# Two value-into-weight foldings per row of small products in the second stage

## The chip, the cores and the metric

One Trainium2 chip, one core. The metric is device time of one execution in microseconds (us); lower is better.

## What is computed

For each of 8 batches of 576 tokens (4608 tokens, 8 heads of 64, width 512) a linear attention with 32 memory slots is computed, and its result goes through two feed-forward layers:

```python
a = softmax over s of phi;  k_m, v_m = a.T @ k, a.T @ v      # per batch and head: 32 x 64
p = softmax((q @ k_m.T) / 8)                                  # per head: 576 x 32
x = concat over heads of p @ v_m                              # 4608 x 512
x = (silu(x @ w_gate) * (x @ w_val)) @ w_out                  # d_ff 1536
out = elu(x @ w_in) @ w_out2                                  # d_ff 2048
```

All is float32. Products that must be exact to float32 are done as three fast products of a high and a low part (`hi*hi + hi*lo + lo*hi`).

## The kernel before, in words

The kernel never forms `p @ v_m`. Since `(p @ v_m) @ w` is `p @ (v_m @ w)`, it folds the 32x64 values of each head into the gate and value weights first. One **folding** (`vw`, line 253) serves one batch `b` and one **unit pair** `p`: two hidden units of 128, gate and value, 512 columns. It is a row of eight small products (64 rows by 32 columns of the array each, one for each head, line 260). They are plain float32, and each shows as two instructions, so a folding is 16 matmul records on line 260. The result fills a PSUM tile of two banks (`pvw`); ScalarE then copies it to a high part (line 265) and VectorE subtracts that from the PSUM tile to get the low part (line 266). Only after the subtraction is the PSUM tile free. `together` (line 95) keeps the products of one row next to each other in TensorE's order.

The program has three stages. The first (lines 593 to 670) does the attention and the first 4 hidden units of the first layer, batch by batch. **The second** (lines 676 to 853) does the other 8 hidden units, and that is where the change is. The third (from line 855) is the second layer.

The second stage goes over four pairs of batches `n`. In each pair there are 8 unit pairs, that is 16 units. A unit (`unit2`, line 698) is 12 matmuls `pg`, a Silu on ScalarE, 12 matmuls `pv`, and a multiplication on VectorE (line 703). After each second unit of `n` comes one folding for the unit pair two further on (line 828). The first 16 units run without output steps around them. From then on the units of `n + 1` are mixed with the 14 **output steps** of `n` (`step`, line 750): each step has two halves `hf`, each of 12 matmuls `acc` (lines 286 to 288), preceded by a high and low split of its input on ScalarE and VectorE (lines 767 and 768). This part is called the mixed stretch below. At the end the 14 steps of the last pair of batches run alone.

PSUM in the second stage: four two-bank tiles, numbered 0 to 3 (`bank2`, line 686). In the mixed stretch the output steps hold 2 and 3, while `pg`, `pv` and the foldings take turns on 0 and 1, in the order of the list `turn` (line 690). In the first 16 units, the units take turns on 0, 1 and 2 (the very first on 3), and foldings use 3 alone.

ScalarE and VectorE also convert the later weights from 64-bit words in the background (`load_w`, `set_split`; lines 127 to 132, 168 and 227 to 233), which fills what time they have left.

The order on each engine is set by a list scheduler while the program is built; it takes the ready instruction of the highest priority. `tc.issue_after(ins)` puts the instructions of a block behind `ins` on the same engine; `high_priority` moves them ahead. An output step is kept behind the unit before it (`behind`, line 754), but only the first three matmuls of a step are.

Of the kernel before, what the change touches and what calls it, by code (L numbers as in the profile page):

```python
# [8 lines left out]
F32 = mybir.dt.float32  # L9
F32R = mybir.dt.float32r  # L10
# [3 lines left out]
ALU = mybir.AluOpType  # L14
# [7 lines left out]
KD = DM // 128  # L22
# [16 lines left out]
def attention_moe_moe(ctx: ExitStack, tc: tile.TileContext, qT, phiT, kv, kv4, w1g, w1o, w2, out):  # L39
# [3 lines left out]
    stt = nc.vector.scalar_tensor_tensor  # L43
    mm = nc.tensor.matmul
# [5 lines left out]
    vx_p = ctx.enter_context(tc.tile_pool(name="vx", bufs=4))  # L50
# [33 lines left out]
    last, first = {}, {}  # L84
# [10 lines left out]
    def together(calls):  # L95
        first = calls[0]()
        with tc.issue_after(first.ins), tc.high_priority():
            for call in calls[1:]:
                call()
# [70 lines left out]
    WG = [[None] * KD for _ in range(NU1 // 2)]  # L170
# [77 lines left out]
    VW = {}  # L248
# [1 line left out]

    def vw(b, p, pool=None, ps=None):
        t = VW[b, p] = vx_p.tile([128, 2, 2, 512], F32R, tag="vx", name="vw")
        both = ps or pool.tile([128, 2, 512], F32, tag="at", name="pvw")
        ps = [both[:, g] for g in range(2)]

        def head(j, g):
            r, c = slice(64 * g, 64 * g + 64), slice(32 * j, 32 * j + 32)
            return mm(ps[g][c], lhsT=Bs[b].vt[r, j, :], rhs=WG[p][j][r], start=True, stop=True)  # L260

        together([lambda j=j, g=g: head(j, g) for j in reversed(range(KD)) for g in (1, 0)])
        if b >= NEG or p >= UA // 2:
            with tc.high_priority() if pool is None else nullcontext():
                act(out=t[:, 0], in_=both, func=AF.Copy)
                tt(out=t[:, 1], in0=both, in1=t[:, 0].bitcast(F32), op=ALU.subtract)
            return
        for g in range(2):
            last["vwh"] = act(out=t[:, 0, g, :], in_=ps[g], func=AF.Copy)
        for g in range(2):  # L270
            mm(ps[g], lhsT=minus, rhs=t[:, 0, g, :], start=False, stop=True, skip_group_check=True)
            last["vwl"] = act(out=t[:, 1, g, :], in_=ps[g], func=AF.Copy)
            if g == 0:
                last["vwl0"] = last["vwl"]
# [10 lines left out]
    def down(ps, w, hs, ms, start, stop, skip=False):  # L285
        mm(ps, lhsT=w[0][:, ms], rhs=hs[0], start=start, stop=False, skip_group_check=skip)  # L286
        mm(ps, lhsT=w[1][:, ms], rhs=hs[0], start=False, stop=False, skip_group_check=skip)  # L287
        mm(ps, lhsT=w[0][:, ms], rhs=hs[1], start=False, stop=stop, skip_group_check=skip)  # L288

    def split_h(pool, h, n):  # L290
        hh = pool.tile([128, n], F32R, tag="hh", name="hh")
# [201 lines left out]
    Bs = [Batch(b) for b in range(B)]  # L493
# [99 lines left out]
    for b in range(B):  # L593
# [53 lines left out]
        hs = {}  # L647
        for hf in range(2):
            for u in range(UA):
                s = gate1(b, u, Bs[b].at, HS * hf, silu)  # L650
# [35 lines left out]
    def bank2(i, name):  # L686
        return (ps_3 if i == 3 else ps_2[i // 2]).tile([128, 2, T], F32, tag=f"g{i}", name=name)

    MIX = 1000
    turn = ([3, 0] + [1, 2, 0] * 10 + [1, 0] * MIX)[:32 + MIX]  # L690

    def up2(b, u, c, name):
        ps = bank2(turn.pop(0), name)
        for hf in range(2):
            up1(ps[:, hf, :HS], VW[b, u // 2], 256 * (u % 2) + c, at2[b], HS * hf)
        return ps[:, :, :HS]

    def unit2(b, u, out):
        pg = up2(b, u, 0, "pg")
        s = t_p.tile([128, 2, HS], F32, tag="s", name="s")  # L700
        last["gate"] = act(out=s, in_=pg, func=AF.Silu)
        pv = up2(b, u, 128, "pv")
        last["h"] = stt(out=out, in0=s, scalar=1.0, in1=pv, op0=ALU.mult, op1=ALU.mult)

    def vw2(b, p):
        if len(turn) > MIX:
            ps = bank2(3, "pvw")
        else:
            ps = bank2(turn.pop(0), "pvw")
        vw(b, p, ps=ps)  # L710


    held = {}
# [33 lines left out]
    def down_steps(n, g, steps, comb):  # L747
        acc = {}

        def step(j, name, r, k, chain, *dst):  # L750
            start = name in ("P1", "P2", "P5", "P4")[:4 if steps is ALONE else 3]
            if start and j == 0:
                acc[chain] = [bank2(i, "acc")[:, :, :HS] for i in ((0, 1) if chain == "D" else (2, 3))]
            behind = nullcontext() if steps is ALONE else tc.issue_after(unit_end[-LAG].ins)
            if steps is not ALONE:
                w = wo_p.tile([128, 2, 2, 256], F32R, tag="w", name="ws")
                nc.sync.dma_start(out=w.bitcast(F32), in_=d1_d[:, r, 2 * j:2 * j + 2])
            else:
                if j == 0:
                    acc["w"] = vx_p.tile([128, 4, 2, 256], F32R, tag="vx", name="ws")  # L760
                    last["ws"] = nc.sync.dma_start(out=acc["w"].bitcast(F32), in_=d1_d[:, r])
                w = acc["w"][:, 2 * j:2 * j + 2]
            for hf in range(2):
                hs = [hs_p.tile([128, 2, HS], F32R, tag=t, name=t) for t in ("hh", "hl")]
                x = g[k][:, hf, 2 * j:2 * j + 2]
                with tc.high_priority():
                    act(out=hs[0], in_=x, func=AF.Copy)  # L767
                    last["h"] = last["gate"] = tt(out=hs[1], in0=x, in1=hs[0].bitcast(F32), op=ALU.subtract)
                for o, a, b, f in comb.get((name, 2 * j + hf), []):
                    with tc.issue_after(last["h"].ins):  # L770
                        tt(out=g[o][:, f], in0=g[a][:, f], in1=g[b][:, f], op=ALU.add if (o, a, b) == (2, 2, 3) else ALU.subtract)
                for i, m in [(i, m) for i in range(2) for m in range(2)]:
                    with behind if hf + i + m == 0 else nullcontext():
                        down(acc[chain][m][:, hf], (w[:, i, 0], w[:, i, 1]), (hs[0][:, i], hs[1][:, i]),
                             slice(128 * m, 128 * m + 128), start and j + i == 0, j + i == 2, not start)
            if j == 1:
                add_part(acc[chain], [(2 * n + b, c) for b, c in dst],
                         name == "P4" if steps is ALONE else None)

        return [lambda a=a, j=j: step(j, *a) for a in steps for j in range(2)]  # L780

    def fetch_x():
# [19 lines left out]
    def background(fs, x):  # L802
        store_w2()
        while fs and len(fs) > x:
            fs.pop(0)()

    pairs = [(2 * n + bi, UA // 2 * (k + 1) + j) for n in range(B // 2) for k in range(2) for bi in range(2)
             for j in range(UA // 2)]
    load2(1)

    unit_end = []
    LAG = 1

    def units(n, g):
        fs, n0 = conv[n], len(conv[n])
        done = [0]

        def unit(i, k, u):
            b, p = pairs[8 * n + i]
            if u % UA == 0:  # L820
                g[k] = gh_p.tile([128, 2, UA, HS], F32, tag="gh", name="gh")
            unit2(b, u, g[k][:, :, u % UA])
            unit_end.append(last["pe"])
            done[0] += 1
            background(fs, n0 * (1 - done[0] / (12 if n == 0 else 16)))
            if u % 2 == 1:
                if 8 * n + i + 2 < len(pairs):
                    vw2(*pairs[8 * n + i + 2])
                if i in (5, 7) and n < B // 2 - 1:
                    load2(2 * n + 2 + i // 7, nc.gpsimd)  # L830

        return [lambda i=i, k=i // 2 % 2 * 2 + i // 4, u=2 * pairs[8 * n + i][1] + j: unit(i, k, u)
                for i in range(8) for j in range(2)]

    g = [{} for _ in range(B // 2)]
# [144 lines left out]
    for q in range(NQD):  # L980
        with tc.issue_after(last["ws"].ins):
            w = fetch(up_d[q][:, 2:6])
        ps = [bank((2 * q + i) % 6) for i in range(2)]
# [7 lines left out]
    for q in range(NQD):  # L991
        w = fetch(dn_d[q // 4][:, 2:6, q % 4])
# [21 lines left out]
    for t0 in range(T, NT, 2 * T):  # L1014
# [10 lines left out]
        def head(q):  # L1025
            z = Q[q]
            z["w0"] = fetch(up_d[q][:, :4])
            z["p1"], z["p5"] = bank(q % 2), bank(3 + 2 * (q % 2))
            product(q, "P1", z["p1"], True)
            with tc.high_priority():  # L1030
                z["s1"] = keep(z["p1"])
            product(q, "P5", z["p5"], True)
            with tc.high_priority():
                z["s5"] = keep(z["p5"])
# [43 lines left out]
        acc = {"D": [dbank(0), dbank(1)]}  # L1078
        K = {}
        for n, (name, r, slot) in enumerate(STEPS):  # L1080
# [3 lines left out]
            start = name in ("P1", "P2", "P5")  # L1084
            for p in range(NQD // 2):
                if p % 2 == 0:
                    w = fetch(dn_d[p // 2][:, r])
                g = G[p]
                hi, lo = split2(g[:, slot], op_p, ("hi", "lo"))
                if name in AFTER:  # L1090
                    o, a, b, op = AFTER[name]
# [10 lines left out]
            for mt in range(2):  # L1102
                ps = acc[chain][mt]
# [52 lines left out]
```

## Time and profile before

| | us |
|---|---|
| median of 3 runs | 1428.58 (1428.11 to 1428.69) |
| the profiled execution's own time | 1427.93 |
| its span | 1426.2 |
| TensorE matmul busy | 1401.3 (98%) |
| VectorE busy | 1136.1 (80%) |
| ScalarE busy | 862.4 (60%) |
| granted TensorE clock, mean of the span | 0.995 |

PE is TensorE's matmul side, PEld its weight loads, DVE is VectorE, ACT is ScalarE, POOL is GpSimd and SP the engine that issues most DMAs. Matmuls are pipelined: one starts while the one before still drains, so the time that a matmul costs is read from the distance between starts, not from its duration. In a timeline each row has the start and the duration in us, the engine, the source line, the operation, output<-inputs by name, and how many instructions were merged; in brackets stands the idle time before it and what ended that.

### The profile page before, as it was taken

The page shows a single profiled execution, that of the slowest core. Times are in us where ns is not written, and L with a number is a line of the kernel's source. Part 1 is how long each engine was busy: PE and PEld are TensorE (multiplying, and loading weights), DVE is VectorE, ACT ScalarE, POOL GpSimd, SP SyncE. Part 2 cuts the span into 40 slices and gives each one's busy share as a digit, 9 for nine tenths or more (in the row PEclk, how much of TensorE's full clock was granted, in tenths as well). Part 3 has the DMA queues.
Part 4 walks back from the last instruction along what each step waited for, and adds up shares of the span by engine and source line. Part 5 has one row for each costly group of instructions (what it writes and reads, how often), then busy time and mean ns, then how long its engine had stood idle before and what let it go on. Part 6 is the DMA issues. An engine that isn't in the chain of part 4 may idle for free.

```text
span 1426.2 us, 23205 instructions
## 1 busy us (share of the span) xinstructions
PE 1401.3 (98%) x9259; PEld 1211.6 (85%) x9259; DVE 1136.1 (80%) x1452; ACT 862.4 (60%) x1254; POOL 44.8 (3%) x73
## 2 busy tenths in 40 slices
PE   6899999999999999999999999999999999999998
PEld 4787889988999999999988888888888888888887
DVE  7988978778798877877988578885889488957884
ACT  5665545544465555555666388557866587548843
POOL 0000000000000000000000000000000000000000
PEclk8999999999999999999999999999999999999999
DMA  9888512664789887888889756766686667566653
GB/s 378 326 298 292 208 72 101 230 233 175 237 251 309 284 240 232 274 241 287 267 291 364 269 188 206 280 214 189 201 282 219 190 202 265 215 210 203 213 201 132
DMA packets 89484, 337.65 MB, mean 237 GB/s; under 512 B 9376, under 2 KB 23712, under 8 KB 70048
## 3 DMA queue, kind: packets, MB, share of 16 engines
q1 hardware_dynamic: 55312, 254.04, 51.6%
q10 hardware_dynamic: 26880, 51.39, 9.8%
q0 software_dynamic: 7184, 30.74, 8.9%
q8 instruction: 73, 1.20, 0.3%
q14 instruction: 35, 0.29, 0.1%
HBM read 251.13 MB, written 85.00 MB: 236 GB/s over the span
## 4 chain that ended last, share of the span: by engine, by line
PE 93%; DVE 3%; ACT 2%; DMA 1%; issue 1%; ACTq 0%; SPq 0%; DVEq 0%
PE pu L877 12%; PE pu L879 12%; PE pu L878 12%; PE pd L877 5%; PE pd L879 5%; PE pd L878 5%; PE acc L288 4%; PE acc L286 4%; PE acc L287 4%; PE pv L281 3%; PE pg L281 3%; PE pv L283 3%; PE pv L282 3%; PE pg L283 3%; PE pg L282 3%; PE pvw L260 3%
## 5 line engine op out<-in xcount | busy, mean ns | idle before, releaser
L878 PE MATMUL pu<-xlo,w 128*128 128x512 f32 x672 | 261.4, 389 | 0.0
L877 PE MATMUL pu<-xhi,w 128*128 128x512 f32 x672 | 261.4, 389 | 0.0
L879 PE MATMUL pu<-xhi,w 128*128 128x512 f32 x672 | 261.4, 389 | 0.0
L906 ACT ACTIVATE xhi<-g 128x1024 fp32r<-128x1024 f32 x120 | 126.5, 1058 | 106.9 <-PE pu L879 64.3
L907 DVE TENSOR_TENSOR xlo<-g,xhi 128x1024 fp32r<-128x1024 f32 x120 | 145.0, 1220 | 40.7 <-ACT xhi L906 40.6
L879 PEld LDWEIGHTS pu<-xhi,w 128*128 128x128 f32 x672 | 126.1, 188 | 26.3
L878 PEld LDWEIGHTS pu<-xlo,w 128*128 128x128 f32 x672 | 126.1, 188 | 26.2
L877 PEld LDWEIGHTS pu<-xhi,w 128*128 128x128 f32 x672 | 126.1, 188 | 26.1
L287 PE MATMUL acc<-hh,ws 128*128 128x288 f32 x448 | 131.7, 296 | 0.0
L286 PE MATMUL acc<-hh,ws 128*128 128x288 f32 x448 | 131.5, 295 | 0.0
L288 PE MATMUL acc<-hl,ws 128*128 128x288 f32 x448 | 128.8, 297 | 0.0
L281 PE MATMUL pv<-at,vw 128*128 128x288 f32 x384 | 115.6, 301 | 2.4 <-DVE s L306 0.7
L281 PE MATMUL pg<-at,vw 128*128 128x288 f32 x384 | 116.7, 304 | 1.1 <-ACT p L579 0.5
L767 ACT ACTIVATE hh<-gh 128x576 fp32r<-128x576 f32 x112 | 76.0, 685 | 68.6 <-PE acc L287 50.8
L282 PE MATMUL pg<-at,vw 128*128 128x288 f32 x384 | 114.1, 297 | 0.9 <-DVE at L488 0.9
L283 PE MATMUL pg<-at,vw 128*128 128x288 f32 x384 | 113.6, 296 | 0.0
L282 PE MATMUL pv<-at,vw 128*128 128x288 f32 x384 | 113.6, 296 | 0.0
L283 PE MATMUL pv<-at,vw 128*128 128x288 f32 x384 | 113.5, 296 | 0.0
L877 PE MATMUL pd<-xhi,w 128*128 128x512 f32 x288 | 112.0, 389 | 0.0
L878 PE MATMUL pd<-xlo,w 128*128 128x512 f32 x288 | 112.0, 389 | 0.0
L879 PE MATMUL pd<-xhi,w 128*128 128x512 f32 x288 | 112.0, 389 | 0.0
L897 DVE SCALAR_TENSOR_TENSOR et<-et 128x1024 f32<-128x1024 f32 x72 | 87.8, 1219 | 28.8 <-ACT et L896 28.8
(161 smaller groups left out, 3226.9 us busy)
## 6 DMA issues: line engine op xcount, KB each, us to landing
w<-dnd SPq DMA_DIRECT2D x64, 1024.0 KB, 4.9
w<-upd SPq DMA_DIRECT2D x40, 1024.0 KB, 5.7
w<-upd SPq DMA_DIRECT2D x32, 768.0 KB, 4.6
ws<-d1d SPq DMA_DIRECT2D x42, 512.0 KB, 4.5
kvr<-kv SPq DMA_DIRECT2D x32, 512.0 KB, 7.5
wr<-w SPq DMA_DIRECT2D x16, 1024.0 KB, 6.3
upd<-uw ACTq DMA_DIRECT2D x32, 512.0 KB, 6.3
dnd<-uw ACTq DMA_DIRECT2D x32, 512.0 KB, 7.9
```

Of the source, the lines that this page charges most:

```text
L281: mm(ps, lhsT=wh, rhs=ah, start=g == 0, stop=False)
L282: mm(ps, lhsT=wh, rhs=al, start=False, stop=False)
L283: last["pe"] = mm(ps, lhsT=wl, rhs=ah, start=False, stop=g == 1)
L286: mm(ps, lhsT=w[0][:, ms], rhs=hs[0], start=start, stop=False, skip_group_check=skip)
L287: mm(ps, lhsT=w[1][:, ms], rhs=hs[0], start=False, stop=False, skip_group_check=skip)
L288: mm(ps, lhsT=w[0][:, ms], rhs=hs[1], start=False, stop=stop, skip_group_check=skip)
L877: mm(ps, lhsT=w[0], rhs=x[0], start=start, stop=False, skip_group_check=skip)
L878: mm(ps, lhsT=w[0], rhs=x[1], start=False, stop=False, skip_group_check=skip)
L879: last["mm"] = mm(ps, lhsT=w[1], rhs=x[0], start=False, stop=stop, skip_group_check=skip)
L897: stt(out=a, in0=e, scalar=1.0, in1=a, op0=ALU.add, op1=ALU.mult)
L906: last["hi"] = act(out=hi, in_=x, func=AF.Copy)
L907: last["lo"] = tt(out=lo, in0=x, in1=hi.bitcast(F32), op=ALU.subtract)
```

## The change

The eight small products and the two evacuation instructions of a folding are taken apart (`vw_calls`, `vw_out`). `vw2` now takes two unit pairs, puts their sixteen small products into one `together`, and then issues both evacuations. It is called after every fourth unit, not after every second. With `n` = 0 it is called at once. In the mixed stretch the two pairs are put into the list `folds`, and the next output step calls `vw2` between its two halves, behind the last `acc` matmul of the first half (TensorE's instructions) and behind the last unit's multiplication (VectorE's). The two foldings of a row then take both PSUM tiles 0 and 1: first the one of the last `pv`, then the one of the last `pg`; the next `pg` takes the tile of the row's first folding and the next `pv` that of the second. With `n` = 0 the first folding of a row takes its turn with the units, and the second takes tile 3.

```diff
-    def vw(b, p, pool=None, ps=None):
-        t = VW[b, p] = vx_p.tile([128, 2, 2, 512], F32R, tag="vx", name="vw")
-        both = ps or pool.tile([128, 2, 512], F32, tag="at", name="pvw")
-        ps = [both[:, g] for g in range(2)]
+    def vw_calls(b, p, ps):
         def head(j, g):
             r, c = slice(64 * g, 64 * g + 64), slice(32 * j, 32 * j + 32)
-            return mm(ps[g][c], lhsT=Bs[b].vt[r, j, :], rhs=WG[p][j][r], start=True, stop=True)
-        together([lambda j=j, g=g: head(j, g) for j in reversed(range(KD)) for g in (1, 0)])
+            return mm(ps[:, g][c], lhsT=Bs[b].vt[r, j, :], rhs=WG[p][j][r], start=True, stop=True)
+        return [lambda j=j, g=g: head(j, g) for j in reversed(range(KD)) for g in (1, 0)]
+
+    def vw(b, p, pool=None, ps=None):
+        both = ps or pool.tile([128, 2, 512], F32, tag="at", name="pvw")
+        together(vw_calls(b, p, both))
+        vw_out(b, p, both, pool)
+
+    def vw_out(b, p, both, pool=None):
+        t = VW[b, p] = vx_p.tile([128, 2, 2, 512], F32R, tag="vx", name="vw")
+        ps = [both[:, g] for g in range(2)]
         if b >= NEG or p >= UA // 2:
             with tc.high_priority() if pool is None else nullcontext():
                 act(out=t[:, 0], in_=both, func=AF.Copy)
...
-        mm(ps, lhsT=w[0][:, ms], rhs=hs[1], start=False, stop=stop, skip_group_check=skip)
+        last["acc"] = mm(ps, lhsT=w[0][:, ms], rhs=hs[1], start=False, stop=stop, skip_group_check=skip)
...
-    turn = ([3, 0] + [1, 2, 0] * 10 + [1, 0] * MIX)[:32 + MIX]
+    turn = ([3, 0] + [1, 2, 0] * 12)[:36] + [0, 1] * (MIX // 2)
...
-        last["h"] = stt(out=out, in0=s, scalar=1.0, in1=pv, op0=ALU.mult, op1=ALU.mult)
-    def vw2(b, p):
-        if len(turn) > MIX:
-            ps = bank2(3, "pvw")
-        else:
-            ps = bank2(turn.pop(0), "pvw")
-        vw(b, p, ps=ps)
+        last["pv"] = last["h"] = stt(out=out, in0=s, scalar=1.0, in1=pv, op0=ALU.mult, op1=ALU.mult)
+    def vw2(*of):
+        at = [turn.pop(0), 3] if len(turn) > MIX else [turn.pop(0) for _ in range(3)][1::-1]
+        ps = [bank2(i, "pvw") for i in at]
+        together([c for bp, t in zip(of, ps) for c in vw_calls(*bp, t)])
+        for bp, t in zip(of, ps):
+            vw_out(*bp, t)
...
                 for i, m in [(i, m) for i in range(2) for m in range(2)]:
+                    if hf == 1 and i + m == 0 and folds:
+                        with tc.issue_after(last["acc"].ins), tc.issue_after(last["pv"].ins):
+                            vw2(*folds)
+                        folds.clear()
                     with behind if hf + i + m == 0 else nullcontext():
...
             if u % 2 == 1:
-                if 8 * n + i + 2 < len(pairs):
-                    vw2(*pairs[8 * n + i + 2])
+                if i % 2 == 0 and n == 0:
+                    vw2(*pairs[i + 2:i + 4])
+                elif i % 2 == 0:
+                    folds.extend(pairs[8 * n + i + 2:8 * n + i + 4])
```

## Rows read from the trace of the kernel before

**Rows 1.** The page: busy us (share) xinstructions of each engine; the chain that ended last.
```profile
PE 1401.3 (98%) x9259; PEld 1211.6 (85%) x9259; DVE 1136.1 (80%) x1452; ACT 862.4 (60%) x1254; POOL 44.8 (3%) x73
...
PE 93%; DVE 3%; ACT 2%; DMA 1%; issue 1%; ACTq 0%; SPq 0%; DVEq 0%
```
**Rows 2.** Windows: length, busy PE, PEld, DVE, ACT, POOL (x), clock, DMA share, GB/s.
```profile
284.00:372.00 88.00, 86.58 (x702) 77.78 (x701) 68.97 (x91) 41.74 (x67) 1.22 (x2) 1.00 0.62 219
372.00:690.00 318.00, 317.76 (x2542) 295.23 (x2541) 261.06 (x339) 178.46 (x270) 20.36 (x25) 1.00 0.86 261
```
**Rows 3.** Waits of PE, 284 to 690 us: total us, times, longest.
```profile
PE pv L281 <- ACT s L701: 0.5, 1, 0.5
PE pv L281 <- ACT p L579: 0.5, 1, 0.5
PE pvw L260 <- DVE vw L266: 0.3, 1, 0.3
```
**Rows 4.** The same windows for line 260 alone: length, busy PE (x), PEld (x).
```profile
284.00:372.00 88.00, 8.72 (x128) 1.45 (x128) 1.00 0.62 219
372.00:690.00 318.00, 23.96 (x352) 3.98 (x352) 1.00 0.86 261
```
**Rows 5.** Timeline of PE around one folding of the mixed stretch.
```profile
540.92 0.30 PE L286 MATMUL acc<-hh,ws 128*128 128x288 f32 x1
541.05 0.29 PE L287 MATMUL acc<-hh,ws 128*128 128x288 f32 x1
541.28 0.66 PE L260 MATMUL pvw<-wg,vt 64*32 64x512 f32 x8
...
541.73 0.64 PE L260 MATMUL pvw<-wg,vt 64*32 64x512 f32 x8
542.30 0.40 PE L288 MATMUL acc<-hl,ws 128*128 128x288 f32 x1
542.53 0.29 PE L286 MATMUL acc<-hh,ws 128*128 128x288 f32 x1
```
**Rows 6.** Timeline of PE in the first stage: rows of small products.
```profile
54.93 0.72 PE L445 MATMUL ps_sc<-qr,kT 64*32 64x288 f32 x16
55.44 1.06 PE L260 MATMUL pvw<-wg,vt 64*32 64x512 f32 x16
56.44 0.33 PE L380 MATMUL ps_aT<-ident,ph 128*128 128x128 f32 x1
...
58.88 0.71 PE L445 MATMUL ps_sc<-qr,kT 64*32 64x288 f32 x16
59.52 0.40 PE L282 MATMUL pv<-at,vw 128*128 128x288 f32 x1
```
**Rows 7.** Timeline: the two evacuations of the folding of rows 5.
```profile
542.47 1.02 ACT L265 ACTIVATE vw<-pvw 128x1024 fp32r<-128x1024 f32 x1 [0.26 <-PE pvw L260]
...
543.88 1.21 DVE L266 TENSOR_TENSOR vw<-pvw,vw 128x1024 fp32r<-128x1024 f32 x1
```
**Rows 8.** Timeline of PE after it: first of 12 pg, first of 19 acc, first pv.
```profile
542.80 0.29 PE L281 MATMUL pg<-at,vw 128*128 128x288 f32 x1
...
544.38 0.29 PE L288 MATMUL acc<-hl,ws 128*128 128x288 f32 x1
...
546.91 0.30 PE L281 MATMUL pv<-at,vw 128*128 128x288 f32 x1
```
**Rows 9.** Timeline: the mixed stretch's folding whose PSUM tile came free last.
```profile
422.35 1.09 PE L260 MATMUL pvw<-wg,vt 64*32 64x512 f32 x16
...
424.86 1.23 DVE L168 TENSOR_TENSOR uq<-uq,wc 128x1024 f32<-128x1024 f32 x1
426.00 1.22 DVE L266 TENSOR_TENSOR vw<-pvw,vw 128x1024 fp32r<-128x1024 f32 x1
```
**Rows 10.** Waits of PEld, 372 to 690 us: total us, times, longest.
```profile
PEld pv L281 <- DVE vw L266: 0.7, 2, 0.4
```

More of the change, by code (lines that the diff above doesn't have):

```diff
@@ L811, in attention_moe_moe @@
     unit_end = []
+    folds = []
     LAG = 1
```

## The prediction

> **What bounds the kernel now.** I read the page first: TensorE is busy for 98% of the span and makes 93% of the chain that ended last; VectorE is the next, at 80% [rows 1]. Then the windows of the second stage: in the mixed stretch TensorE is busy for 317.76 of 318 us at the full granted clock, VectorE for 261.06 [rows 2]. A busy TensorE can still be a slow one, since a busy time is made of pipelined durations, so I went on to its waits: from 284 to 690 us they name 1.3 us in all [rows 3]. The timeline confirms it: ordinary 288-column matmuls start every 0.13 us (12 `pg` from 542.80 to 544.38, 0.132 each [rows 8]). So this stretch is a queue of TensorE work without holes, and what is taken out of that queue moves all that follows, unless a new wait takes its place. Stage three is bound by TensorE as well, by the same page.
>
> **What a folding costs now.** From the start of the last ordinary matmul ahead of one (541.05) to the start of the second one behind it (542.53) are 1.48 us [rows 5]. Two ordinary steps of 0.133 are in that, so the folding costs 1.21 us. Its parts: the first small product starts 0.23 after the matmul ahead of it (0.10 more than an ordinary step); the first eight records take 0.45 until the second eight start (541.28 to 541.73); those take 0.57 until the next ordinary matmul (541.73 to 542.30); and that one takes 0.23 until its follower, again 0.10 more than normal. Two groups of eight at 0.45 would be 0.90; the other 0.31 to 0.32 (0.10 + 0.12 + 0.10, with rounding) is paid for going from full-size matmuls to the small tiles and back.
>
> **The change, part by part.**
>
> *Sixteen products in one row.* Line 260 has 128 records in the window up to 372 us and 352 behind it, at 16 a folding 8 and 22 foldings [rows 4]. They become 4 and 11 rows, so 15 changes to small tiles and back go away. No row here shows two foldings together, so I bound the price of one such joint. The low end takes just the two delays next to ordinary matmuls, 0.10 + 0.10 = 0.20 us, as if the longer last group stayed. The middle takes the group as well, 0.31. The high end comes from the nearest thing in the trace, a score row that runs straight into a folding: there the folding starts 0.51 after the score row does (54.93 to 55.44), while a score row that is followed by an ordinary matmul takes 0.64 (58.88 to 59.52); the joint saves 0.13 of that, the 0.10 behind the row and the 0.10 ahead of the folding, and the folding itself takes 1.00 where it took 1.02 (55.44 to 56.44 [rows 6], against 541.28 to 542.30 [rows 5]): 0.35. This high end is the same kind of joint with the same tile size, so I take 0.33, nearer to it than to the low end. 15 x 0.33 = 5.0 us saved, between 3.0 and 5.3.
>
> *Evacuations.* They are as many as before and as long (1.02 us on ScalarE, 1.21 on VectorE [rows 7]), and neither engine is full [rows 2]. No DMA is added, removed or moved past another on SP's or POOL's queue; the steps' loads and the loads of `at2` stay where they were, relative to units and steps. Cost nothing by themselves, as long as the next `pg` has something in front of it.
>
> *Both PSUM tiles at once.* This is the new wait. Today a folding takes one of the two tiles that `pg` and `pv` use; the other serves the next `pg` at once (542.80, half a microsecond after the folding [rows 8]). Afterwards the next `pg` needs the tile of the row's first folding. In the typical case of rows 7 the tile is free at 545.09, 2.72 us after the folding's last product ended (541.73 + 0.64 = 542.37). In a row, the first folding is through about 0.90 (two groups) before the second, so its tile is free 1.8 us after the row's end. In front of `pg` stands the second half of the output step, 12 matmuls x 0.133 = 1.6 us. This leaves a hole of 0.2 us at most rows if nothing else is put there. The bounds: none, if ScalarE and VectorE follow without delay (1.02 + 1.21 and the 0.10 until ScalarE begins is 2.3, less 0.9 is 1.4, under 1.6); and 1.3 us in the worst case seen, where conversion instructions sat in VectorE's queue ahead of the subtraction, the last of them the one of 424.86: folding's end 423.44, tile free at 427.22, 3.78 us, less 0.9 is 2.9 [rows 9]. Such holes have been filled so far: after the folding of rows 5 the scheduler put 19 `acc` matmuls, 2.5 us, between `pg` and `pv`, just while the tile was not free [rows 8]; where it didn't, the weight loads of a `pv` waited for the subtraction, twice in this stretch and 0.7 us in all [rows 10]. Of the next step only 3 of 24 matmuls must stand behind the unit, so there is filler. The `pv` behind it has 1.6 us more; the second tile comes one subtraction (1.21) later: no new hole. I charge 0.05 us on the average for 11 rows, 0.5 us, with 0 and 14 (1.3 x 11) as ends.
>
> *Waiting at the row's start.* The first folding needs the last unit's multiplication done, and VectorE's two subtractions queue behind that multiplication. The first half of the step, 1.6 us of `acc`, lies in between, and the multiplication takes 0.75; the row may slip into the step's second half if it isn't ready. Nothing is charged; if the cover is gone, the price is in the ends above. What queues behind the two subtractions (2.4 us) on VectorE is the next step's low split; it is made a half step ahead, and is what would be late next.
>
> *The first 16 units.* Foldings that now run early in tile 3 come later, after every fourth unit; they are needed two units (6.4 us) behind the row. Here the units have three tiles, and the row's first tile comes round again after two groups of 12, 3.2 us after the row's end, against 1.8 to 2.9: nothing. VectorE's delays already cost TensorE some 1.4 us here (88 less 86.58 [rows 2]); they may shift, by less than 1 either way.
>
> **The sum.** -5.0 + 0.5 = -4.5 us against the profiled execution's own 1427.93 (span 1426.2): 1423.4. The median of the runs is 0.65 above that execution, so the forecast for the median of the changed kernel is 1424.1.
>
> The Trainium skill speaks against it (TensorEngine Tiling, section PSUM Bottleneck): packing speeds up the matmuls and not the emptying of PSUM, which then may be the bottleneck. By that rule the row's two subtractions would set the pace, and the outcome would be the first rival's, 1428.0; the waits of rows 10 say that so far they do not.
>
> **The rivals.**
>
> *The gain is given back at PSUM.* The scheduler finds no filler, and each of the 11 mixed rows waits between the typical 0.2 and the middle of the ends (0.65), say 0.4: 4.4 us lost of 5.0, 1428.0. For it: the wait of rows 10 exists today with one folding. Against: it happens at 2 of 22, and VectorE is idle for 18% of the stretch.
>
> *Slower: VectorE's queue.* A conversion instruction of 1.2 us stands ahead of the first subtraction of each mixed row, as in rows 9: 0.2 + 1.2 = 1.4 us, half of it filled by `acc`: 0.7 x 11 = 7.7 us lost, 5.0 gained, 1431.3. It decides against the change from 0.45 us a row on (5.0 / 11). For it: VectorE's order is fixed ahead, and two evacuations now come at once. Against: rows 9 show the worst of 22, and in rows 7 the subtraction began 0.4 us after its input was there (542.47 + 1.02 to 543.88).
>
> *The row doesn't join.* The second folding waits in mid row for its tile, or other matmuls get between: no change to small tiles is saved, 1428.6. Against: the tile of the last `pg` was read by Silu long before.
>
> **How the numbers follow.** Some 0.2% (2.9 us) is what a measurement of this kernel can tell from no change. Forecast 0.66, from 1422.9 (5.3 saved, and some of today's waits gone) to 1425.7; given back at PSUM 0.17; doesn't join 0.07; slower 0.10. Faster 0.66, same 0.24, slower 0.10. A range from 1422.9 to 1428.2 leaves out the slower rival, the upper part of the same cases and a little below.
>
> **What would show it.** Right: line 260 in 15 groups of 32 records from the second stage on, each some 0.33 us shorter than two foldings (2.09 us for a row, not 2 x 1.21 = 2.42); the stretch up to the last unit shorter by 4 to 5 us; no new wait on line 266. Wrong: PE waits of `pg` on line 266 that sum to more than 1 us, groups of 16, or a joint that saves under 0.2.

## The result, and the profile after

The changed kernel takes **1439.43 us** (median of 6 runs, 1438.07 to 1440.67), the kernel before 1428.34 beside it: a ratio of 1.0078, 95% interval 1.0065 to 1.0091. It is 11 us slower where 4.5 us less were forecast. The profiled execution took 1439.45 us, its span 1437.7.

Line numbers have moved: small products 260 to 257, a folding's copy and subtraction 265 and 266 to 271 and 272, `pg` and `pv` 281 to 283 to 287 to 289, `acc` 286 to 288 to 292 to 294.

The page first; the columns are those of [rows 1].

```profile
PE 1401.2 (97%) x9259; PEld 1216.1 (85%) x9259; DVE 1138.3 (79%) x1452; ACT 862.5 (60%) x1254; POOL 45.5 (3%) x73
...
PE 85%; DVE 6%; DMA 4%; ACT 2%; issue 2%; ACTq 0%; SPq 0%; DVEq 0%
```

Busy time is the same to 0.4% on TensorE (with its weight loads), VectorE and ScalarE, yet TensorE's share of the chain that ended last fell from 93 to 85%, and VectorE's doubled. Time went into waiting. The windows of the second stage show where (the mixed stretch now ends some 11 us later, so its window is 10 us longer than in [rows 2]):

```profile
284.00:372.00 88.00, 85.41 (x701) 78.01 (x700) 68.84 (x91) 41.45 (x66) 1.23 (x2) 1.00 0.62 220
372.00:700.00 328.00, 318.25 (x2526) 298.64 (x2525) 261.07 (x336) 176.95 (x268) 20.95 (x25) 0.98 0.84 252
```

TensorE stands still for 9.75 of 328 us of the mixed stretch, where it stood still for 0.24 before, and its granted clock is 0.98 there, not 1.00. The waits of PE from 284 to 700 us, the same view as in [rows 3], show what it waits for:

```profile
PE pg L287 <- DVE vw L272: 9.7, 7, 3.0
PE pg L287 <- ACT s L707: 0.8, 1, 0.8
PE pv L287 <- ACT p L585: 0.7, 2, 0.5
PE acc L292 <- ACT ev L735: 0.4, 2, 0.2
PE pv L287 <- DVE vw L272: 0.4, 1, 0.4
```

The next `pg` waits for VectorE's subtraction of a folding: 9.7 us in seven waits, five of them, with 7.9 us, in the mixed stretch. The prediction had named more than 1 us of such waits as a sign that it is wrong. What these `pg` need are the row's two tiles, which are held until the subtraction is through.

**The joint itself came out as forecast.** This is PE's timeline around one row, to be read like [rows 5]:

```profile
520.65 0.43 PE L294 MATMUL acc<-hl,ws 128*128 128x288 f32 x2
521.01 1.95 PE L257 MATMUL pvw<-wg,vt 64*32 64x512 f32 x32
522.89 0.40 PE L292 MATMUL acc<-hh,ws 128*128 128x288 f32 x1
523.13 0.30 PE L293 MATMUL acc<-hh,ws 128*128 128x288 f32 x1
```

The two merged `acc` start at 520.65 and 0.133 later, at 520.78. From there to 523.13 are 2.35 us; less two ordinary steps of 0.133 that is 2.08 us for two foldings, against 2 x 1.21: 0.34 saved from these rounded times, 0.36 from the unrounded starts (I took 0.33).

**The worst hole.** The timeline around the row of 489 us, all engines (lines of the stretch left out):

```profile
489.18 1.95 PE L257 MATMUL pvw<-wg,vt 64*32 64x512 f32 x32
...
490.27 1.14 ACT L232 ACTIVATE uw<-uq 128x512 fp32r<-128x512 f32 x2
...
490.90 1.35 DVE L777 TENSOR_TENSOR gh<-gh 128x1152 f32<-128x1152 f32 x1
491.31 1.93 ACT L271 ACTIVATE vw<-pvw 128x1024 fp32r<-128x1024 f32 x2
492.17 1.28 DVE L233 TENSOR_TENSOR uw<-uq,uw 128x512 fp32r<-128x512 f32 x2
...
493.38 1.35 DVE L777 TENSOR_TENSOR gh<-gh 128x1152 f32<-128x1152 f32 x1
...
494.65 2.34 DVE L272 TENSOR_TENSOR vw<-pvw,vw 128x1024 fp32r<-128x1024 f32 x2
```
```profile
492.63 0.29 PE L294 MATMUL acc<-hl,ws 128*128 128x288 f32 x1
495.91 0.61 PE L287 MATMUL pg<-at,vw 128*128 128x288 f32 x1 [2.99 <-DVE vw L272]
```

The row ends at 491.06, and the 12 `acc` behind it end at 492.76. ScalarE converts first (490.27) and copies the first folding only at 491.31; by 492.33 its high part is there. VectorE, whose order is fixed, then still has a conversion pair and a combination (L777, sums of `gh` for the output steps) ahead of the subtraction, which starts at 494.65. `pg` starts at 495.91: a hole of 3.15 us. The same pattern stands at 600 us.

What follows each of these two holes can be read from the windows of 489 to 502 us and of 600 to 611.5 (granted clock in the third column from the end), and from matmuls behind each hole:

```profile
489.00:496.00 7.00, 4.01 (x47) 2.22 (x46) 7.00 (x9) 4.78 (x8) 0.85 (x1) 0.92 0.92 268
496.00:502.00 6.00, 6.00 (x26) 6.00 (x27) 0.99 (x1) 0.65 (x1) 0.00 (x0) 0.52 0.57 203
600.00:606.60 6.60, 3.65 (x44) 2.03 (x44) 6.60 (x9) 4.63 (x7) 0.85 (x1) 1.00 0.97 278
606.60:611.50 4.90, 4.85 (x25) 4.86 (x26) 1.12 (x1) 0.65 (x1) 0.00 (x0) 0.65 0.78 259
```
```profile
499.20 0.45 PE L288 MATMUL pv<-at,vw 128*128 128x288 f32 x1
499.44 0.45 PE L289 MATMUL pv<-at,vw 128*128 128x288 f32 x1
...
607.27 0.30 PE L288 MATMUL pg<-at,vw 128*128 128x288 f32 x1
607.41 0.33 PE L289 MATMUL pg<-at,vw 128*128 128x288 f32 x1
...
608.01 0.45 PE L289 MATMUL pg<-at,vw 128*128 128x288 f32 x1
608.25 0.45 PE L287 MATMUL pg<-at,vw 128*128 128x288 f32 x1
```

Around each of these two holes the granted clock falls to the lower of its two levels (1.2 GHz): matmuls start every 0.24 us, not every 0.133. At the first hole it has fallen by the time the `pg` starts; at the second the first matmuls still start every 0.13 us (607.27 to 607.41), and 0.9 us after the hole it falls. No shorter hole of this kernel's second stage was followed by that.

**Where there was filler.** Rows differ in what stands behind them. Counted in PE's order, five of the 11 mixed rows have 24 `acc` between the row and the next `pg`, and none of the five has a hole at that `pg`, though the first tile came free only 1.9 to 2.8 us behind the row's end. One of them is the row of 521.01:

```profile
526.06 0.29 PE L294 MATMUL acc<-hl,ws 128*128 128x288 f32 x1
526.19 0.30 PE L287 MATMUL pg<-at,vw 128*128 128x288 f32 x1
```

The other six have 10 to 12 `acc`, as the row of 489 us, and all six have a hole there: 0.2 to 0.4 us at three, where the tile came free after 1.7 to 2.0 us, and 1.56, 3.15 and 3.15 at the three where it came after 3.1, 4.7 and 4.7.

**The account.** I call a hole the time by which the distance between two starts on PE exceeds the ordinary 0.133 us, where that distance is over 0.246; ahead of a row and behind it, what exceeds the ordinary distance there counts too. "Mixed holes" are those of the mixed stretch. Added up: first 16 units 2.0 us before, 3.4 after; mixed holes 0.6 before, 11.8 after. That is 12.6 us more. Matmuls at the lower clock cost some 4.3 us more. 15 joints at 0.34 to 0.36 give 5.1 to 5.4 back. Sum +11.5 to +11.8; the last `pv` starts 11.5 us later (680.97 before, 692.42 after). Ahead of the second stage, where the scheduler's order changed as well, the changed kernel had gained 0.4 us (the last score row starts at 196.79, before at 197.22); the account is no finer than that.

### The profile page after: what moved, and what is told of

It reads as the page before. It is cut to its first block, busy times and chain, and to the rows that moved or that the text cites. A ratio compares the mean times of both kernels' runs of the same rounds, so it can differ in the third digit from the quotient of the medians.

```text
span 1437.7 us, 23188 instructions
## 1 busy us (share of the span) xinstructions
PE 1401.2 (97%) x9259; PEld 1216.1 (85%) x9259; DVE 1138.3 (79%) x1452; ACT 862.5 (60%) x1254; POOL 45.5 (3%) x73
## 4 chain that ended last, share of the span: by engine, by line
PE 85%; DVE 6%; DMA 4%; ACT 2%; issue 2%; ACTq 0%; SPq 0%; DVEq 0%
PE pu L890 12%; PE pu L892 12%; PE pu L891 12%; PE pd L890 5%; PE pd L892 5%; PE pd L891 5%; PE acc L292 4%; PE acc L293 4%; PE acc L294 4%; PE pg L287 3%; PE pv L287 3%; PE pg L289 3%; PE pg L288 3%; PE pv L288 3%; PE pv L289 3%; PE pd L292 2%
```

## The experiments

The theory: a joint row takes both PSUM tiles of the units, and the loss is the next `pg`'s wait until VectorE has subtracted. Each run is the changed kernel with one edit, unless said; times stand beside the kernel before, run with it (1426.9 to 1428.0 us).

**The place, without the joining.**

```diff
-        at = [turn.pop(0), 3] if len(turn) > MIX else [turn.pop(0) for _ in range(3)][1::-1]
+        at = [turn.pop(0), 3] if len(turn) > MIX else [turn.pop(0) for _ in range(3)][1::-1] if len(of) > 1 else [turn.pop(0)]
...
-                elif i % 2 == 0:
-                    folds.extend(pairs[8 * n + i + 2:8 * n + i + 4])
+                elif n and 8 * n + i + 2 < len(pairs):
+                    folds.append(pairs[8 * n + i + 2])
```


> The changed kernel, but in the mixed stretch each folding is a row of its own again, still in the middle of an output step and behind the same two instructions; the first 16 units keep their joint rows. Theory (both PSUM tiles of the units are taken at once, and the next pg waits for VectorE's subtraction): the 11.8 us of holes of the mixed stretch fall under 1.5 us and the half clock behind the two longest goes, while 11 joints at 0.33 us are lost; what is left of the holes of the first 16 units, 1.8 us more than before, against 4 joints, 1.3 us, gives 1428 to 1430 us. Rival (the place in the middle of the step, behind acc and behind the last multiplication, costs the time, not the joining): the holes stay, 1436 us or more.

1430.66 us, ratio 1.002 (1.0011 to 1.003). The mixed holes are 3.1 us, no more `pg` waits on a folding there, and the clock stays up. In the mixed stretch all that PE waits for is this:

```profile
PE pv L287 <- DVE vw L272: 2.6, 3, 1.0
```

So the place in the step costs little by itself; joining there costs 9 us. (My range was missed by 0.7: three `pv` waits of 0.9 were not foreseen.) The place isn't the same throughout, though: the scheduler put 6 to 36 `acc` between the last `pv` and a single folding, and 12 to 26 ahead of a joint row.

**The place, with the joining.** The row issued straight after the units:

```diff
-                if i % 2 == 0 and n == 0:
-                    vw2(*pairs[i + 2:i + 4])
-                elif i % 2 == 0:
-                    folds.extend(pairs[8 * n + i + 2:8 * n + i + 4])
+                if i % 2 == 0 and 8 * n + i + 2 < len(pairs):
+                    vw2(*pairs[8 * n + i + 2:8 * n + i + 4])
```


> The changed kernel, but in the mixed stretch the joint row is issued straight after the fourth unit, as the single foldings were before, without the two instructions that it has to stay behind; the scheduler places it. Theory (two tiles at once): the next pg still needs a tile of the row, so holes of 5 to 12 us stay; 1433 to 1440 us. Rival (the place in the step is the cost): the holes go and the joints are kept, 1423 to 1427 us.

1436.82 us (ratio 1.0061, 1.0046 to 1.0076); mixed holes 10.3 us, as the theory has it. It is a weak test of the place: by the count of `acc` ahead of a row and behind it, 7 of the 11 rows stand where they stood, since the scheduler puts a row behind the output step's matmuls unasked.

**What runs ahead of the subtractions.**

```diff
+                if hf == 1 and folds:                       # ahead of the combinations
+                    with tc.issue_after(last["acc"].ins), tc.issue_after(last["pv"].ins):
+                        vw2(*folds)
...
                 for o, a, b, f in comb.get((name, 2 * j + hf), []):
-                    with tc.issue_after(last["h"].ins):
+                    with tc.issue_after(last["h"].ins), tc.issue_after(last.get("fold", last["h"]).ins):
...
-        for after in last.get("h"), first.get("ex"):        # later(): the conversions
+        for after in last.get("h"), first.get("ex"), last.get("fold"), last.get("foldc"):
```


> The changed kernel, but the combinations of the same half step are issued after the row and kept behind its subtractions on VectorE, and the conversions issued later than a row are kept behind its copies on ScalarE and behind its subtractions on VectorE. Nothing is left out. Theory (the two tiles at once cost time mainly because combinations and conversions stand ahead of the subtractions): the two holes of 3.15 us, where a combination, two conversion instructions and another combination ran ahead of the subtractions, fall under 1 us each with the half clock behind them; 1429 to 1434 us. Rival (two evacuations in a row are too long for the half step's cover whatever stands ahead): holes stay over 10 us in all, 1436 us or more.

1433.47 us (ratio 1.0041, 1.0026 to 1.0056). The two holes of 3.15 fall to 0.88 each, and the mixed holes from 11.8 to 8.2. A hole of 2.1 us stands at 411 us instead, where just 6 `acc` follow the row, and the clock is at its lower level for 3.5 us around it. The waits of the mixed stretch:

```profile
PE pg L287 <- DVE vw L272: 6.1, 6, 1.9
PE pv L287 <- DVE vw L272: 0.4, 1, 0.4
```

The result lies between the two expectations. The order is worth 6 us with the clock that goes with it, and half of the loss stays. The edit does not reach what still runs ahead: on ScalarE the emptying of output steps and conversions issued before the row, on VectorE the other half of those conversions.

**The cover.** These two moved the row in the source, half a half step later and earlier:

```diff
-                    if hf == 1 and i + m == 0 and folds:
+                    if hf == 1 and i == 1 and m == 0 and folds:    # late
+                    if hf == 0 and i == 1 and m == 0 and folds:    # early
```


> The changed kernel with the row half a half step later: 6 of the step's 24 matmuls follow it, not 12, so 0.8 us less work covers its evacuations. Theory (cover against the time until the tile is free): each of the 7 or so rows that leave a hole now leaves 0.8 us more, and the four that just fit begin to; 5 to 9 us more than the change, 1444 to 1449 us. Rival (only what VectorE and ScalarE run ahead of the evacuations decides, the cover is taken up by filler anyway): within 2 us of the change, 1437 to 1442 us.

> The changed kernel with the row half a half step earlier: behind the first 6 matmuls of the step, so that 18 follow it, 0.8 us more cover. Theory: the 7 rows with holes lose 0.8 us each at most, 3 to 6 us in all, and half clock may go with them: 1432 to 1437 us. Rival (the row then waits for the last unit's multiplication, which has 0.8 us of cover, not 1.6, and what is gained behind the row is lost ahead of it): 1438 to 1442 us.

1438.62 and 1439.48 us: the change again. They tested nothing: at all 11 rows as many `acc` stand ahead and behind as in the change. In PE's timeline of the first mixed row of the early kernel, 12 `acc` matmuls stand behind the row and none of the 6 more that the edit asked for:

```profile
383.71 1.95 PE L257 MATMUL pvw<-wg,vt 64*32 64x512 f32 x32
385.59 0.40 PE L292 MATMUL acc<-hh,ws 128*128 128x288 f32 x1
...
387.16 0.29 PE L294 MATMUL acc<-hl,ws 128*128 128x288 f32 x1
388.86 0.40 PE L287 MATMUL pg<-at,vw 128*128 128x288 f32 x1 [1.40 <-DVE vw L272]
```

Its `pv` ends 24 `acc` ahead of the row, as in the change. The scheduler had put those `acc` ahead of the row. What holds the row there wasn't tried; the row also needs the last `pv`'s tile, and for that VectorE's multiplication.

**Early and behind, and the first 16 units.** The row early and the order edit together (the combinations now behind the matmuls of their half step); then also single foldings into tile 3 for `n` = 0, as before the change.

```diff
-    turn = ([3, 0] + [1, 2, 0] * 12)[:36] + [0, 1] * (MIX // 2)
+    turn = ([3, 0] + [1, 2, 0] * 10)[:32] + [1, 0] * (MIX // 2)
...
+                if n == 0: vw2(pairs[i + 2])        # at = [3]
```


> The row early and, as in the kernel that keeps combinations and later conversions behind the subtractions, nothing of those ahead of the evacuations; the combinations come behind the matmuls of their half step. Theory: cover and order are two terms of one sum, and what is left of the mixed stretch's holes (8.2 us with the order alone) falls by 0.8 us at each of the 8 rows that have one: under 3.5 us; 1427 to 1430 us. Rival (one of the two makes up for the other): the same as the better of the two alone, 1432 to 1435 us.

> The same, but the first 16 units fold one pair at a time into tile 3 again, as before the change. Theory: their holes go back from 3.4 to 1.6 us and 4 joints at 0.33 us are lost: 0.5 us less than with joint rows there, 1426.5 to 1429.5 us; the kernel before is 1428. Rival (the single foldings there cost more than the holes): 1 us more.

1435.67 and 1435.71 us. The first is just above the rival's range; the second equals the first, so neither its theory nor its rival came out. Nothing adds up (mixed holes 10.6 and 11.6 us). Single foldings in the first 16 units do take their holes from 4.2 back to 2.3 us, but the mixed stretch, whose source is the same, got 1.0 us more. Reordering one part moves the other.

**Filler behind the row.** Rows in steps 0, 4, 8, 12; then with the order edit and single foldings for `n` = 0.

```diff
-                elif i % 2 == 0:
-                    folds.extend(pairs[8 * n + i + 2:8 * n + i + 4])
...
+            if i in (0, 4, 8, 12):
+                at = 8 * n + 10 + 2 * (0, 4, 8, 12).index(i)
+                folds.extend(pairs[at:at + 2])
```


> The changed kernel, but the rows of the mixed stretch go into steps 0, 4, 8 and 12, not 1, 5, 9 and 13. An odd step is the last of its product: behind its 12 remaining matmuls ScalarE must empty the output tiles before the next step can begin, so nothing can fill a wait; behind an even step stands the second step of the same product, into the same tiles, with 21 matmuls that need not wait for the unit. Theory (the holes are as long as they are because the row stands where there is no filler): the mixed stretch's holes fall from 11.8 to under 5 us, 1429 to 1434 us. Rival (the row itself waits for the tile of the last pv, so the filler is used up ahead of it, wherever it stands): holes over 9 us, 1436 us or more.

> Rows in the even steps, combinations and later conversions kept behind the subtractions, and one folding at a time into tile 3 in the first 16 units: what each theory leaves as the best. Theory (filler and order add up): mixed holes under 3 us against 11 joints, 3.6 us: 1425 to 1429 us, level with the kernel before or a little under it. Rival (the row uses up the filler): as the order alone did, 1432 to 1436 us.

1438.11 and 1443.54 us: the rival's, and worse. The mixed holes are 11.5 and 15.9 us, now at nearly every row. In the first of the two, PE's waits of the mixed stretch are:

```profile
PE pg L287 <- DVE vw L272: 9.0, 9, 1.6
```

No wait is as long as 3 us, but there are nine. This does not show that filler is no help, because the edit brought none: between a row and the next `pg` stand 2 to 12 `acc`, and 24 to 32 between the last `pv` and the row. The scheduler used the filler up ahead of the row, as the rival has it. The row of 433.07, with two `acc` behind it:

```profile
433.07 1.95 PE L257 MATMUL pvw<-wg,vt 64*32 64x512 f32 x32
...
435.18 0.29 PE L294 MATMUL acc<-hl,ws 128*128 128x288 f32 x1
437.12 0.45 PE L287 MATMUL pg<-at,vw 128*128 128x288 f32 x1 [1.64 <-DVE vw L272]
```

Here first tiles came free 1.5 to 2.8 us behind a row's end, about the 1.8 to 2.9 of the prediction, and too little stood in front of `pg` to cover them.

**Letting go of the tile without VectorE.** First as a measurement that leaves out the low parts of the second stage's folded weights:

```diff
-                tt(out=t[:, 1], in0=both, in1=t[:, 0].bitcast(F32), op=ALU.subtract)
+                lo_src = both if pool is not None else t[:, 0].bitcast(F32)
+                tt(out=t[:, 1], in0=lo_src, in1=t[:, 0].bitcast(F32), op=ALU.subtract)
```


> The changed kernel, but in the second stage VectorE's subtraction of a folding reads the high part twice, out of SBUF, and not the PSUM tile. It leaves out the low parts of those weights (they come out as zero); all instructions stay, and the PSUM tile is free as soon as ScalarE has copied it. Theory (both tiles are held until VectorE's subtractions are through, and that is where the changed kernel loses): the pg waits on line 272 go, what is left of the mixed stretch's holes is ScalarE's and under 3 us (11.8 in the change), no half clock; the joints' 5.0 us come out, and with the holes of the first 16 units gone as well the time is 1422 to 1426 us. Rival (ScalarE's copies alone are late enough, being behind its other work by up to 1.9 us): 3 to 8 us of holes stay, 1427 to 1433 us. Rival (the loss does not hang on the tiles): 1437 us or more.

> The kernel before with the same edit: it leaves out the low parts of the second stage's folded weights. It shows what the edit is worth where only one tile is taken at a time. Theory: the two holes of 0.28 us behind a subtraction go, and some of the waits of the first 16 units: 1426.5 to 1428.5 us. Rival (a subtraction that reads SBUF alone is itself worth much): 1425 us or less.

**1423.05 us** for the changed kernel (ratio 0.997, 0.9959 to 0.998), 1430.85 for the kernel before with the same edit (1.0018, 1.0008 to 1.0028). The mixed stretch of the first has no hole left, at the full clock; its window, then one of VectorE's subtraction pairs, behind a row that started at 484.98:

```profile
372.00:690.00 318.00, 318.00 (x2576) 300.90 (x2575) 265.73 (x343) 179.07 (x273) 20.95 (x25) 1.00 0.87 268
```
```profile
484.98 1.95 PE L257 MATMUL pvw<-wg,vt 64*32 64x512 f32 x32
...
487.11 1.93 ACT L271 ACTIVATE vw<-pvw 128x1024 fp32r<-128x1024 f32 x2
490.45 2.35 DVE L273 TENSOR_TENSOR vw<-vw 128x1024 fp32r<-128x1024 f32 x2
```

All instructions are there and the subtractions take the same 1.2 us each. They come late as ever, 5.47 us behind the row's start here (484.98 to 490.45) as at the worst row of the change (489.18 to 494.65), behind the same instructions in VectorE's order, and nobody waits for them. This is the run that decides: with the order around that row unchanged and VectorE's hold gone, the holes go, and the change gains 4.9 us. That this is nearly the forecast's 5.0 is in part luck. The joints give 5.4 us and the 0.6 us of mixed holes go as well, but the first 16 units have 4.1 us of holes, 2.1 more than before the change; with the 0.4 us gained ahead of the second stage that makes 4.3 of the 4.6 us by which the third stage's first product starts earlier (719.94, before at 724.50). The edit alone gains nothing where one tile is taken at a time; there it lost 2.5 to 3 us. Its trace has two waits for that, at 317 and 362 us, neither of them on a folding's tile: a Silu that ScalarE ran behind a conversion and a folding's copy, and the DMA of an output step's weights. Behind the second the clock is at its lower level for 3.4 us.

```profile
PE acc L287 <- DMA ws<-d1d: 2.7, 1, 2.7
PE pv L282 <- ACT s L702: 1.6, 1, 1.6
```

**Which tile.** The same edit for the first folding of each row alone (half of those low parts left out).

```diff
+                lo_src = t[:, 0].bitcast(F32) if sb else both      # sb: first of the row
```


> The changed kernel, but the subtraction of the first folding of each row of the second stage reads the high part twice, out of SBUF; that of the second folding reads PSUM as before. It leaves out the low parts of half of those weights (they come out as zero). Theory (the tile of the next pg, the row's first, costs it): nearly all of the mixed stretch's 11.8 us of holes go; 1422.5 to 1426 us. Rival (both tiles cost about the same, since the pv has only 1.6 us more): 4 us of holes or more stay, at pv; 1428 to 1434 us.

1433.2 us (ratio 1.0041, 1.0026 to 1.0056): the rival's range, and 8.0 us of mixed holes. The `pg` waits on a folding go, and `pv` waits for the second tile in their place. More than that is a second `pg`, which the scheduler put ahead of the late `pv`: its tile is held by a Silu that ScalarE ran behind conversions and the emptying of an output tile. The waits of the mixed stretch:

```profile
PE pg L288 <- ACT s L708: 3.8, 3, 1.6
PE pv L288 <- DVE vw L273: 2.2, 3, 0.9
PE acc L293 <- ACT ev L736: 0.4, 2, 0.2
```

**With nothing left out.** ScalarE copies the folding unrounded to SBUF and the parts are made from there: for all foldings, into the conversions' output pool; then for the first of a mixed row alone, into a buffer of its own, for which that pool went from 4 to 3; then that with single foldings for `n` = 0.

```diff
+            rw = rw_p.tile([128, 2, 512], F32, tag="rw", name="rw")     # or up_p, tag "u"
+            act(out=rw, in_=t0, func=AF.Copy)
+        vw_out(*bp1, t1)
+        vw_out(*bp0, rw)
```


> The changed kernel, but in the second stage ScalarE first copies a folding out of PSUM unrounded (into a tile of the conversions' output pool), and the high and low parts are made from that copy: one more ScalarE instruction of about 1.03 us for each of 30 foldings, and the PSUM tile is free without VectorE. Theory (the wait for VectorE's subtraction is the loss): the first tile is free about 0.3 us after the row's end, the second 1.0 us later, both before pg and pv want them; the holes of the mixed stretch fall to under 3 us and the time to 1424 to 1429 us. Rival (ScalarE's own queue, with the splits of the output steps in it, is as late as VectorE's): the pg waits go over to ScalarE's copy and the time stays above 1434 us. Rival (the place in the step): 1438 us or more, since ScalarE has more to do.

> The changed kernel with nothing left out: in the mixed stretch ScalarE first copies the row's first folding unrounded out of PSUM into a buffer of its own (one; the conversions' output pool goes from 4 buffers to 3 to make room), then makes the second folding's high part, then the first's from the copy; VectorE subtracts the second from PSUM and the first from the copy. One ScalarE instruction of 1.03 us more for each of 11 rows. Theory (the wait is for VectorE at the first tile): mixed holes under 2 us, 1423 to 1427 us, faster than the kernel before. Rival (ScalarE's longer queue or the conversions' lost buffer makes new waits): 1429 us or more.

> The same, with one folding at a time into tile 3 in the first 16 units, as before the change. Theory (there a joint row gains 1.3 us and costs 1.8 us of holes): 0.5 us under the run with joint rows there, 1422.5 to 1426.5 us. Rival (the holes there come from VectorE's conversions and not from the rows): 1.3 us over it.

1447.66, 1446.71 and 1444.75 us. All are slower, and not for one reason. In the first, three waits of `pg` on the new copy make 15 us, 7.7 the longest; ScalarE ran conversions ahead of that copy, and the copy itself waited 0.65 us for a buffer that was still being stored. In the second, PE's two longest waits of the mixed stretch, and then ACT's longest that was not there in the change, are:

```profile
PE pv L287 <- DVE vw L272: 5.8, 5, 1.7
PE acc L292 <- ACT ev L744: 5.2, 3, 4.8
```
```profile
ACT uw L232 <- DMA upd<-uw: 10.9, 3, 5.3
```

ScalarE stands 5.3 us before a conversion whose output buffer is still being stored, and with it, in the same queue, the emptying of the output step's tiles. The `pv` waits are those of the run before: the second tile still hangs on VectorE. A version that copies both foldings out and keeps all four buffers of the pool was not run (a buffer is 4 KB a partition), so whether ScalarE alone could pay for the gain stays open.

## Why the prediction was wrong

- **Right: what bounds the kernel, and the price of a joint.** TensorE's mixed stretch had 0.6 us of holes in 318, 15 joints came to 0.34 to 0.36 us each (0.33 taken), and with VectorE's hold gone the change does gain. That the gain is 4.9 us against a sum of 5.0 is in part luck (see the run above).
- **Wrong: the charge for "both PSUM tiles at once".** 0.05 us a row, 0.5 us, was taken; the mixed stretch paid 11.2 us in holes (11.8 less 0.6) and some 4 at the lower clock. The end of that term, 14 us, was in the text, and the range did not take it in.
- The step that failed is the one from the single foldings' delays to a row's, and the filler set against it. I took the delay from folding to free tile (2.7 typical, 3.8 worst [rows 7, 9]) as it was with one subtraction to place, which gave 1.8 and 2.9 for a row. Eight of the 11 rows kept to that (1.7 to 2.8). At three the first tile came free later, 3.1, 4.7 and 4.7 us behind the end of the row's last product (491.12 to 495.86 at the worst), since ScalarE's and VectorE's orders had conversions and combinations ahead; these three make 7.9 us of the holes. 6 us of the loss went when those issued later were held back. How the rest is shared between the length of two evacuations and what the engines still ran ahead was not taken apart.
- The filler came from an order [rows 8] that had one tile free for `pg`. "Of the next step only 3 of 24 matmuls must stand behind the unit, so there is filler" held at five rows of 11, and those have no hole at `pg`; at the other six only 10 to 12 `acc` stood there, and all six have one. Moving the rows to even steps did not bring filler behind them.
- "The second tile comes one subtraction later: no new hole" was wrong as well. With the first tile free early, `pv` waited in its place (2.2 us in three waits).
- The slower rival had the mechanism: conversions ahead of the subtraction, from 0.45 us a row on. Measured is about 1.0 a row (11.2 / 11) and the clock on top, which no part of the prediction priced. It got 0.10, and its own time, 1431.3, is 8 us short.
- The first 16 units: "nothing" was charged, 1.4 us of holes came. The prediction also put the 1.4 us that TensorE stood still there before down to VectorE; of the 1.3 us that [rows 3] name, ScalarE's Silu and `p` have 1.0.
- The Trainium skill (TensorEngine Tiling (Array Packing), section PSUM Bottleneck) says that tiling speeds up TensorE and not the emptying of PSUM, and that the copy out of PSUM may then become the bottleneck. The trace agrees so far as the new waits, 9.7 us of `pg` on the subtraction, stand at that emptying. It was not VectorE's rate that ran out, though: VectorE is busy for 261.07 of 328 us in the mixed stretch. It was the time for which two tiles at once were held.

## What to carry over

Joining two small jobs on a full engine also joins their buffers' hold times: count how many of the buffers that the next job rotates through are left in the meantime, price the hold with the evacuating engine's whole queue, not with the delay seen when one buffer was taken, and count at each place what work really stands behind it to cover the hold. To find out which hold it is, let the evacuating instruction read something else and look at the time: one run told more than all those that moved the work about. Where a list scheduler makes the order, read the built order before believing that an edit moved anything.

## What was not expected of the hardware

Around the two holes of 3.15 us the granted clock was 0.52 over 496 to 502 us and 0.65 over 606.6 to 611.5, and matmuls of 288 columns started every 0.24 us. So a wait of 3.15 us cost near 5 (5.8 and 4.8). The length of a hole alone did not settle whether that happens: in the run with rows in even steps a hole of 1.8 us at 437 us was followed by it, and in the run with the row straight after the units one of 2.1 us at 496 us was not.

And a subtraction takes 1.22 us whether it reads PSUM [rows 7] or SBUF alone (2.35 for two): on VectorE the source of such a pass made no difference; for TensorE it made all of it.
